# Attention in halves of 64 tokens on 64x64 parts of TensorE's array, in two visits a unit

## The chip, the cores and the metric

The kernel runs on one core of a Trainium2 chip. The metric is device time in microseconds (us). The kernel before took 674.11 us, the median of three runs (673.33 to 675.0).

A core has five engines that each work through their own instructions in order: PE (TensorE, matmuls; PEld are its weight loads), DVE (VectorE), ACT (ScalarE), POOL (GpSimd) and SP, which only issues DMAs here. ACT issues some DMAs too.

## The reference

Three layers follow each other: a linear attention with a decaying state (4 batch rows, 8 heads, 768 tokens, head size 48), a feed-forward layer with a maximum of three products, and a second one with a softmax and a layer norm. The change is in the first.

```python
for t in range(S):
    cur = np.einsum('bhd,bhe->bhde', u[None] * kt, vt)
    y[:, :, t] = np.einsum('bhd,bhde->bhe', rt, state + cur)
    state = wt[:, :, :, None] * state + np.einsum('bhd,bhe->bhde', kt, vt)
...
h = np.maximum(np.maximum(x @ w1, x @ w2), x @ w3);  x = h @ w_out
h = x @ w_in;  e = np.exp(h - h_max);  sm = e / (e.sum() + 1e-09)
solu = h * sm;  ln = (solu - mu) / np.sqrt(var + 1e-06) * g_ln;  out = ln @ w_out
```

## The kernel before

**Units.** The attention goes by 24 units, `u = 0..23`: 128 tokens of one batch row, all 8 heads, in 4 pairs `p` of 2 heads `e`. Units 0 to 3 are the first chunks of the four batch rows (`u // B == 0`), units 20 to 23 the last ones. Partitions 0 to 63 hold the even heads (48 rows used, padded to 64), 64 to 127 the odd ones.

**What a unit does.** DVE scans the products of `w` backwards (`s_sfx`, L265) and forwards (`s_pfx`, L283); POOL multiplies the first into `k` (L268), DVE the second into `r` (`s_rp`, L287). The diagonal (the term with `u`) comes from `s_rk` (POOL), `s_rku` and `s_diag` (DVE), and `s_dg` (POOL, L324) lays it out in two 128x512 tiles, one for each `e`. On PE:

- `s_score` (L336): 8 matmuls, 64 partitions by 128 key tokens by 128 query tokens, into two PSUM tiles. `s_mask` (DVE, L342, once for each `e`) copies what lies under the causal mask over the diagonal's tile.
- `s_y`: where there is a state, 8 matmuls of the decayed state `st` with `r` (L397, 64 by 64, 128 columns), and 8 of `v` with the masked scores (L401, all 128 key tokens by 64, 128 columns), in one accumulation. `s_yT` (ACT, L463) takes it out of PSUM.
- `s_state` (L418): 8 matmuls of the transposed `k` with `v` (128 tokens by 48, 64 columns), not for the last chunk. `s_sadd` adds them to the decayed state (DVE, L432, two instructions; for the first chunk two ACT copies, L434).

The transposed `k` comes from PE for units 0 to 4 (`s_kTp`) and from a DVE transpose and a round trip by DMA for later ones (`s_kq`, `s_kT`).

**Order.** All is issued in one order that is written out by hand. Units 0 to 3 stand in a loop of their own, mixed with the conversion of the first layer's weights (`conv`: three ACT, two DVE and some POOL instructions a piece; L195 and L199 are DVE's). From unit 4 on, each unit is a list of 12 items (`unit_items`), and `run_groups` deals the items out between groups of 9 matmuls of the first feed-forward layer (`stage_a` L526, `stage_b` L545), by PE time. After each 9 of L526, DVE or ACT must take the result out of one of 4 PSUM buffers (`ps_m`); the attention has 4 more (`ps_a`). So PE leaves the feed-forward matmuls three times for each unit: for the scores, for `s_y`, and for `s_state`. After the attention comes the second layer (L777, L854).

fp32 matmuls (the attention's) appear as two records each in the trace; those of the feed-forward layers, in float32r, as one.

Of the kernel before, what the change touches and what calls it, by code (L numbers as in the profile page):

```python
# [15 lines left out]
L = 128  # L16
NC_ = T // L
# [25 lines left out]
FMW = 2 * NP * L + NP * WB  # L43
# [26 lines left out]
def emit(tc, general, flag, fm, tm, ub, wa, win, wo2, g, cst, lmask, out):  # L70
# [7 lines left out]
    with ExitStack() as top:  # L78
# [5 lines left out]
        mask = cs[:, 0:128]  # L84
        ident = flat(x2)[:, KX * NU * L - 128:]
        ps_m = top.enter_context(tc.tile_pool(name="ps_m", bufs=4, space=PS))
        ps_a = top.enter_context(tc.tile_pool(name="ps_a", bufs=4, space=PS))
# [11 lines left out]
        a1 = attn.enter_context(tc.tile_pool(name="a1", bufs=1, side="right"))  # L99

        fm_t, rk_t, v_t, at = {}, {}, {}, {}
        xt, xf = {}, {}

        def parts(u):
            t = fm_t[u]
            p3 = lambda x: x.rearrange("p (a b) -> p a b", a=NP)
            return p3(t[:, 0:NP * L]), p3(t[:, NP * L:2 * NP * L]), t[:, 2 * NP * L:]

        def load_f(u, eng=A):
            """The rows between the heads hold constants that stay in a buffer once they are in it."""  # L110
            if u < NU and u not in fm_t:
                fresh = u < (2 if general else 3)
                fm_t[u] = fbuf[u % 2 if general else u if u < 3 else (u - 3) % 2]
                if u == 0:
                    eng.dma_start(parts(u)[2], fm[u][:, 2 * NP * L:])
                    eng.dma_start(fm_t[u][:, 0:2 * NP * L], fm[u][:, 0:2 * NP * L])
                elif fresh:
                    eng.dma_start(fm_t[u], fm[u])
                else:
                    for o in (0, 64):  # L120
                        eng.dma_start(fm_t[u][o:o + D], fm[u][o:o + D])

        def load_rk(u, eng=A):
            if u < NU and u not in rk_t:
                tag = dict(tag="kq", bufs=1) if u == 2 and not general else dict(tag="tm")
                rk_t[u] = apool.tile([128, 2 * DM], F32, name=f"rk{u}", **tag)
                eng.dma_start(rk_t[u], tm[u][:, 0:2 * DM])

        def load_v(u, eng=A):
            if u < NU and u not in v_t:  # L130
                tag = dict(tag="st", bufs=1) if u == 2 and not general else dict(tag="v")
                v_t[u] = apool.tile([128, H * DV], F32, name=f"v{u}", **tag)
                eng.dma_start(v_t[u], tm[u][:, 2 * DM:])
# [5 lines left out]
        fbuf = [a1.tile([128, FMW], F32, name=f"fm{i}") for i in range(2)] + [flat(x2)[:, SPARE:SPARE + FMW]]  # L139
# [14 lines left out]
        for s in sbd:  # L154
            G.memset(s, 0.0)

# [103 lines left out]
        def s_sfx(u):  # L260
            """Products of w over the tokens after each one, into k."""
# [46 lines left out]
        def a_tile(u, e):  # L308
            if not general and u in (1, 3):
                o = SPARE + FMW + e * NP * L  # L310
                return flat(x2)[:, o:o + NP * L].rearrange("p (a b) -> p a b", a=NP)
            return apool.tile([128, NP, L], F32, tag=f"a{e}", bufs=1, name=f"a{e}_{u}")

        def s_dg(u):
            d = at[u]
            for e in range(2):
                s = bc_last(d["s"].rearrange("p (a b) -> p a b", b=2)[:, :, e], L)
                if general:
                    t = apool.tile([128, NP, L], F32, tag="kq", bufs=1, name=f"dg{e}_{u}")
                    V.tensor_tensor(t, bc_mid(ident, NP), s, op=ALU.mult)  # L320
                    V.tensor_tensor(d["a", e], d["a", e], t, op=ALU.add)
                else:
                    d["a", e] = a_tile(u, e)
                    G.tensor_tensor(d["a", e], bc_mid(ident, NP), s, op=ALU.mult)  # L324

        def s_score(u):
            d = at[u]
# [10 lines left out]
        def s_mask(u, e):  # L338
# [3 lines left out]
            V.copy_predicated(d["a", e], bc_mid(mask.bitcast(I32), NP), d["sc", e])  # L342
# [43 lines left out]

        def s_y(u):
# [4 lines left out]
            s = sbd[u % B] if general else d.get("st")  # L392
# [15 lines left out]

        def s_state(u):
            d = at[u]  # L410
            if u // B == NC_ - 1:
                return
            v = v_t[u]
            d["ds"] = ps = pool_of(u).tile([128, NP, DV], F32, tag=pool_tag(u), name=f"ds{u}")
# [5 lines left out]

        def s_sadd(u):
            d = at[u]
            if u // B == NC_ - 1:
                return
            if general and u // B:
                G.tensor_tensor(sbd[u % B], sbd[u % B], bc_last(d["ptot"], DV), op=ALU.mult)
            for e in range(2):
                o = 64 * e
                dst = sbd[u % B][o:o + D]
                if u // B:  # L430
                    old = dst if general else d["st"][o:o + D]
                    V.tensor_tensor(dst, d["ds"][o:o + D], old, op=ALU.add)  # L432
# [3 lines left out]
        def s_kq(u):  # L436
            if NPT <= u < NU - B:
# [5 lines left out]
        def s_kT(u):  # L443
            if u < NU - B:
# [4 lines left out]
        pool_of = lambda u: ps_m if u < B else ps_a  # L449
        pool_tag = lambda u: "m" if u < B else "a"  # L450

        def s_kTp(u):
            if u < NPT:
                s_kT(u)
                ps = pool_of(u).tile([128, NP, L], F32, tag=pool_tag(u), name=f"kTp{u}")
# [4 lines left out]
        def s_yT(u):  # L460
            ps = at[u]["yp"]
            xf[u] = x = apool.tile([128, NP, L], F32, tag="xf", bufs=1, name=f"xf{u}")
            A.activation(x, ps, AF.Copy)  # L463
# [22 lines left out]
        def unit_items(u):  # L486
            n = u + 1
            nx = lambda f: f(n) if n < NU else None
            return [
                lambda: general and (s_diag(u), s_dg(u)),  # L490
                lambda: (s_score(u), s_kTp(u), s_decay(u)),
                lambda: (s_mask(u, 0), s_mask(u, 1), load_t(u + 1)),
# [7 lines left out]
                lambda: general or nx(s_diag),  # L500
                lambda: (general or nx(s_dg), n >= NPT and nx(s_kT)),
            ]

# [72 lines left out]
        def second_weights():  # L576
            """Ends the attention, with the check of the range of w, and sets up the last weights in its place."""
# [7 lines left out]
            attn.close()  # L585
            w2 = right.enter_context(tc.tile_pool(name="w2", bufs=1, side="right"))
# [19 lines left out]
        nc.sync.dma_start(cs, cst[:, 0:128])  # L606
# [11 lines left out]
        end_of = []  # L618
        for u in range(NU):
            items += unit_items(u)  # L620
            end_of.append(len(items) + 4)
        items += [lambda: None] * 3 + [lambda: s_xt(NU - 1)] + [lambda: None] * LEAD
# [34 lines left out]
        for u in range(B):  # L657
# [17 lines left out]
            if l >= 0:  # L675
# [7 lines left out]
            grp(GRP[u][0])  # L683
            s_y(u)
            conv.dve()
            if l >= 0:
# [12 lines left out]
        s_state(B - 1)  # L699
        s_sadd(B - 1)  # L700
        if general:
            for f in (s_sfx, s_pfx, s_rp, s_rk, s_rku):
                f(B)
        pos = end_of[B - 1] - 4
# [7 lines left out]
        def run_groups(groups, k0, k1, extra=(), ahead=1.0):  # L712
            """Emits MoE groups with attention items k0..k1 and the extra steps spread over them by PE time."""
# [181 lines left out]
def build(tc, fm, tm, ub, wa, win, wo2, g, cst, lmask, out):  # L895
    nc = tc.nc
    args = (fm, tm, ub, wa.bitcast(I32), win.bitcast(I32), wo2.bitcast(I32), g, cst, lmask, out)
# [10 lines left out]
def layout(r, k, v, w, u, moe_w1, moe_w2, moe_w3, moe_w_out, moe2_w_in, moe2_w_out, moe2_g_ln):  # L908
# [30 lines left out]
    cst = np.concatenate([i[:, None] < i[None, :], i[:, None] == i[None, :]], axis=1).astype(f32)  # L939
    lm = []  # L940
# [4 lines left out]
    d = dict(fm=fm, tm=tm, ub=ub, wa=wa, win=win, wo2=wo2, g=g, cst=cst, lmask=lmask)  # L945
# [17 lines left out]
```

## Time and profile before

| | us |
|---|---|
| median of the runs | 674.11 |
| profiled execution, span | 672.6 |
| PE busy | 627.4 (93%) |
| DVE busy | 469.3 (70%) |
| POOL busy | 416.3 (62%) |
| ACT busy | 300.3 (45%) |
| mean granted TensorE clock | 0.974 of full speed |

The profile is one execution on the chip. Busy times of PE are from the modelled ends of pipelined matmuls, so where it is busy all the time only the distance from one start to the next tells what an instruction costs. The granted clock is 1.0 or 0.5 in the records, 2.4 or 1.2 GHz.

### The profile page before, as it was taken

How to read it: one execution, taken by the hardware profiler on the slowest of the kernel's cores; microseconds unless marked ns; L12 is line 12 of the kernel's file. 1: busy time of each engine (PE TensorE's matmuls, PEld its weight loads, DVE VectorE, ACT ScalarE, POOL GpSimd, SP SyncE). 2: the span in 40 equal slices, each digit the busy share in tenths (PEclk: the TensorE clock that was granted, in tenths of full speed). 3: DMA queues.
4: the chain of work that ended last, by engine and by line, in shares of the span. 5: the costliest groups of instructions: out<-in, count | busy, mean ns of one | idle time of the engine just before them, and what ended most of it. 6: DMA issues, size and time to landing. Idle time of an engine off the chain costs nothing.

```text
span 672.6 us, 13761 instructions
## 1 busy us (share of the span) xinstructions
PE 627.4 (93%) x5038; PEld 582.1 (87%) x5038; DVE 469.3 (70%) x835; ACT 300.3 (45%) x738; POOL 416.3 (62%) x571
## 2 busy tenths in 40 slices
PE   1648898999999999999999999999999999999996
PEld 1537787999999999999999999999899999999996
DVE  8996889556688877776666562466877777777750
ACT  3565676122434434322222223475655555555542
POOL 6775678544566655565545553276877777777762
PEclk9877798999999999999999999999999999999998
DMA  9844571644465555455543330330577666676661
GB/s 343 212 121 122 175 176 44 153 110 109 109 144 133 135 146 125 117 111 109 110 110 78 79 80 7 95 99 32 127 156 163 158 150 150 137 160 149 146 153 54
DMA packets 158205, 85.57 MB, mean 127 GB/s; under 512 B 132048, under 2 KB 139984, under 8 KB 158128
## 3 DMA queue, kind: packets, MB, share of 16 engines
q1 hardware_dynamic: 149392, 58.37, 36.1%
q10 hardware_dynamic: 8736, 26.22, 15.3%
q8 instruction: 42, 0.69, 0.4%
q14 instruction: 35, 0.29, 0.2%
HBM read 62.68 MB, written 20.71 MB: 124 GB/s over the span
## 4 chain that ended last, share of the span: by engine, by line
PE 84%; DVE 6%; DMA 3%; issue 2%; ACT 2%; POOL 1%; SPq 1%; ACTq 0%; DVEq 0%
PE a L526 32%; PE h L777 15%; PE o L854 15%; PE b L545 11%; PE y L401 3%; PE sc L336 3%; PE y L397 3%; PE ds L418 1%; DMA v<-in_tm_dram 1%; DVE x L199 1%; DMA rk<-in_tm_dram 1%; DVE x L195 1%; DVE pf L283 1%; DMA fm<-in_fm_dram 1%; DVE sf L265 1%
## 5 line engine op out<-in xcount | busy, mean ns | idle before, releaser
L526 PE MATMUL a<-xh,wah 128*128 128x256 f32 x594 | 173.1, 291 | 1.7 <-DVE t L533 1.7
L526 PE MATMUL a<-xh,wal 128*128 128x256 f32 x594 | 168.8, 284 | 1.4 <-POOL wal L209 1.4
L526 PE MATMUL a<-xl,wah 128*128 128x256 f32 x594 | 168.7, 284 | 0.0
L533 DVE TENSOR_TENSOR t<-a,t 128x256 f32<-128x256 f32 x144 | 60.2, 418 | 92.0 <-PE a L526 70.8
L536 POOL TENSOR_TENSOR h<-t,h 128x256 fp32r<-128x256 f32 x66 | 55.9, 847 | 107.4 <-ACT h L535 103.8
L526 PEld LDWEIGHTS a<-xh,wah 128*128 128x128 f32 x594 | 114.3, 192 | 6.8 <-issue 2.0
L526 PEld LDWEIGHTS a<-xh,wal 128*128 128x128 f32 x594 | 114.4, 193 | 1.8 <-POOL wal L209 1.8
L526 PEld LDWEIGHTS a<-xl,wah 128*128 128x128 f32 x594 | 114.5, 193 | 0.1
L854 PE MATMUL o<-wo,lh 128*128 128x384 f32 x368 | 94.0, 337 | 0.0
L535 ACT ACTIVATE h<-t 128x256 fp32r<-128x256 f32 x66 | 27.5, 417 | 147.0 <-DVE t L533 141.1
L777 PE MATMUL h<-wi,x2h 128*128 128x512 f32 x288 | 90.7, 396 | 0.0
L846 POOL TENSOR_TENSOR ll<-c,lh 128x512 fp32r<-128x512 f32 x44 | 64.7, 1491 | 22.1 <-ACT lh L845 22.1
L545 PE MATMUL b<-h,wbh 128*128 128x256 f32 x396 | 73.6, 287 | 0.0
L854 PEld LDWEIGHTS o<-wo,lh 128*128 128x128 f32 x368 | 66.9, 189 | 1.8
L545 PEld LDWEIGHTS b<-h,wbh 128*128 128x128 f32 x396 | 61.8, 192 | 2.0 <-issue 1.0
L777 PEld LDWEIGHTS h<-wi,x2h 128*128 128x128 f32 x288 | 53.7, 189 | 10.9
L854 PE MATMUL o<-wo,ll 128*128 128x384 f32 x184 | 62.0, 337 | 0.0
L324 POOL TENSOR_TENSOR a<-x,s 128x512 f32<-128x512 f32 x44 | 47.6, 1103 | 18.0 <-DVE s L306 18.0
L777 PE MATMUL h<-wi,x2l 128*128 128x512 f32 x144 | 57.0, 396 | 0.0
L545 PE MATMUL b<-h,wbl 128*128 128x256 f32 x198 | 56.2, 284 | 0.5 <-POOL wbl L209 0.5
L793 ACT ACTIVATE e<-h,sm 128x512 f32<-128x512 f32 x48 | 32.6, 684 | 52.1 <-DVE sm L788 52.0
L794 DVE SCALAR_TENSOR_TENSOR p<-h,e 128x512 f32<-128x512 f32 x48 | 32.6, 691 | 20.3 <-ACT e L793 20.3
(134 smaller groups left out, 1337.8 us busy)
## 6 DMA issues: line engine op xcount, KB each, us to landing
fm<-in_fm_dram ACTq DMA_DIRECT2D x42, 289.5 KB, 5.1
pd<-q SPq DMA_DIRECT2D x23, 512.0 KB, 2.9
c<-pd SPq DMA_DIRECT2D x92, 128.0 KB, 3.8
x<-in_wa_dram SPq DMA_DIRECT2D x24, 384.0 KB, 3.8
rk<-in_tm_dram ACTq DMA_DIRECT2D x21, 384.0 KB, 3.6
v<-in_tm_dram ACTq DMA_DIRECT2D x21, 256.0 KB, 4.3
out_dram<-os SPq DMA_DIRECT2D x24, 192.0 KB, 3.2
kd<-kq SPq DMA_DIRECT2D x15, 256.0 KB, 3.8
```

Source lines behind the costliest of these rows:

```text
L324: G.tensor_tensor(d["a", e], bc_mid(ident, NP), s, op=ALU.mult)
L336: PE.matmul(d["sc", e][:, p], k3[o:o + 64, p], r3[o:o + 64, p], start=True, stop=True)
L526: PE.matmul(ps, w_[:, f, m, k], x_[:, k], start=(i == 0), stop=(i == 8))
L533: V.tensor_tensor(t, ps, t, op=ALU.max)
L535: A.activation(hh[:, f], t, AF.Copy)
L536: G.tensor_tensor(hl[:, f], t, hh[:, f].bitcast(F32), op=ALU.subtract)
L545: PE.matmul(ps, w_[:, f, m * 128:(m + 1) * 128], h_[:, f], start=(f == 0 and i == 0), stop=(f == KF1 - 1 and i == 2))
L777: PE.matmul(ps, x_[:, k], w_[:, k, b * 512:(b + 1) * 512], start=(n_ == 0), stop=(n_ == 8))
L793: A.activation(e[:, sl], d["h"][b], AF.Exp, bias=col(0), accum_out=col(2 + b))
L794: V.scalar_tensor_tensor(p[:, sl], d["h"][b], 1.0, e[:, sl], op0=ALU.mult, op1=ALU.mult, accum_out=col(4 + b))
L846: G.tensor_tensor(ll[:, b], c[:, b], lh[:, b].bitcast(F32), op=ALU.subtract)
L854: PE.matmul(ps, l_[:, k], w_[:, k], start=(n_ == 0), stop=(n_ == 3 * KF2 - 1))
```

## The change

Each unit is cut in halves `j` of 64 tokens. The score of a half against itself is 64x64, so each of the four combinations of `e` (rows of the array) and `j` (columns) is a matmul of its own on a 64x64 part, 64 columns long. What the second half needs of the first no longer stands in the scores: it goes through a second state `st1`, which is the decayed state plus the first half's `k` and `v`. `s_intra` (scores with `v`), `s_state2` and `s_inter` (state with `r`) take the place of `s_y` and `s_state`. In the items of a unit, `s_inter(u-1)` and `s_score(u)` stand together, and `s_intra(u)` and `s_state(u)` stand together.

The diagonal's tile is 128x512 once instead of twice, and so is the mask. `s_state2` is also done for the last chunk (first half only), with its transposed `k`. The loads of `r`, and of `k` and `w`, are two DMAs over all 128 partitions (before: two over 48 partitions each), issued at the third item of a unit instead of the tenth; `s_kq` moves from the ninth to the fourth item, `s_kT` from the twelfth to the eighth. The PSUM pool `ps_a` becomes two pairs of banks, `s` (scores, then state) and `y`, each with one buffer. The mask and the small identity come in one constant `half_cst`.

```diff
         def s_score(u):
-            for e in range(2):
-                d["sc", e] = ps_a.tile([128, NP, L], F32, tag="a", name=f"sc{e}_{u}")
+            d["sc"] = sc = pair("s", f"sc{u}")
             for p in range(NP):
-                for e in range(2):
-                    o = 64 * e
-                    PE.matmul(d["sc", e][:, p], k3[o:o + 64, p], r3[o:o + 64, p], start=True, stop=True)
+                for j in range(2):
+                    t = slice(j * HL, (j + 1) * HL)
+                    for e in range(2):
+                        o = slice(64 * e, 64 * e + 64)
+                        PE.matmul(sc[64 * j:64 * j + 64, e, p], k3[o, p, t], r3[o, p, t], start=True, stop=True)
...
+        def s_intra(u):
...
+            d["yp"] = y = pair("y", f"y{u}")
+            for p in range(NP):
+                for j in range(2):
+                    for e in range(2):
+                        h = 2 * p + e
+                        o = slice(64 * j, 64 * j + 64)
+                        PE.matmul(y[64 * e:64 * e + 64, j, p], v[o, h * DV:(h + 1) * DV], d["a"][o, h],
+                                  start=(p == 0), stop=(c == 0 and j == 0 and p == NP - 1))
+
+        def s_inter(u):
...
+            for j in range(0 if u // B else 1, 2):
+                s = d["st1"] if j else d["st"]
+                for p in range(NP):
+                    for e in range(2):
+                        o = slice(64 * e, 64 * e + 64)
+                        PE.matmul(d["yp"][o, j, p], s[o, p], rt[o, p, j * HL:(j + 1) * HL],
+                                  start=False, stop=(p == NP - 1))
...
+        def s_state2(u):
...
+            d["ds"] = ds = pair("s", f"ds{u}")
+            for p in range(NP):
+                for j in range(1 if u // B == NC_ - 1 else 2):
+                    o = slice(64 * j, 64 * j + 64)
+                    for e in range(2):
+                        h = 2 * p + e
+                        PE.matmul(ds[64 * e:64 * e + 64, j, p], d["kT"][o, p, 64 * e:64 * e + 64],
+                                  v[o, h * DV:(h + 1) * DV], start=True, stop=True)
...
+        def s_sadd2(u):
...
+            d["st1"] = st1 = apool.tile([128, NP, DV], F32, tag="st1", bufs=1, name=f"st1_{u}")
+            if u // B:
+                V.tensor_tensor(st1, d["ds"][:, 0], d["st"], op=ALU.add)
+            else:
+                A.activation(st1, d["ds"][:, 0], AF.Copy)
+            if u // B < NC_ - 1:
+                V.tensor_tensor(sbd[u % B], d["ds"][:, 1], st1, op=ALU.add)
...
+                return [
+                    lambda: (u > B and s_inter(u - 1), s_score(u), s_kTp(u)),
+                    lambda: (s_mask(u), u > B and s_yT(u - 1), s_decay(u), nx(s_sfx)),
+                    lambda: load_f(u + 2),
+                    lambda: (s_intra(u), s_state(u), nx(s_kq), u == B and s_xt(u - 1)),
+                    lambda: (s_sadd(u), load_t(u + 1)),
...
             s_dg(m)
-            s_mask(u, 0)
-            s_mask(u, 1)
+            s_mask(u)
+            grp(GRP[u][0])
+            if general:
+                s_y(u)
+            else:
+                s_intra(u)
+                s_state(u)
+                s_sadd(u)
+                s_inter(u)
```

The first place is PE around unit 6, in the stretch where the items are dealt out. Before, the scores (`sc`), the output (`y`, first with the state `st`, then with `a` and `v`) and the state (`ds`) stand apart, with feed-forward matmuls where lines are left out:

```order
L336 MATMUL sc_6_1283<-fm_97 128x128
L336 MATMUL sc_6_1284<-fm_97 128x128
...
L397 MATMUL y_1354<-fm_97,st_1293 64x128 x8
L401 MATMUL y_1354<-a_6_1239,v_993 64x128
L401 MATMUL y_1354<-a_6_1241,v_993 64x128
...
L418 MATMUL ds_1424<-v_993,kT_1243 48x64 x8
```

On PE at the same place of the changed program, with unit 6's output `y_1489`; the next unit's scores are `sc_1688`:

```order
L424 MATMUL y_1150<-fr_98,st_5_1219 64x64 x8
L350 MATMUL sc_1411<-fr_96,fk_100 64x64 x16
...
L412 MATMUL y_1489<-a_1380,v_1224 64x64 x16
L458 MATMUL ds_1506<-v_1224,kT_1296 64x64 x16
...
L424 MATMUL y_1489<-fr_96,st_1449 64x64 x8
L424 MATMUL y_1489<-fr_96,st_6_1544 64x64 x8
L350 MATMUL sc_1688<-fr_97,fk_99 64x64 x16
```

Three places became two; the second and third matmul of a unit now stand together, and the one with the state follows a unit's length later, in front of the next scores.

The second place is DVE in unit 1, in the loop of the first four units. Before, the two masks are followed by the conversion (`x`) and the next unit's scan (`sf`):

```order
L306 TENSOR_REDUCE s_270<-rk_136 128x8
L342 COPY_PREDICATED x_66<-cs,sc_1_224 128x512
L342 COPY_PREDICATED x_66<-cs,sc_1_225 128x512
L195 SCALAR_TENSOR_TENSOR x_66<-x_66 128x384
L199 SCALAR_TENSOR_TENSOR x_66<-x_66 128x384
```

On DVE of the changed program at that place (`sbd` is the state that the next chunk reads, `st_1` is `st1` of unit 1):

```order
L315 TENSOR_REDUCE s_307<-x_66 128x8
L357 COPY_PREDICATED x_66<-cs,sc_263 128x2x4x64
L484 TENSOR_TENSOR sbd_115<-ds_329,st_1_346 128x256
L204 SCALAR_TENSOR_TENSOR x_66<-x_66 128x384
L208 SCALAR_TENSOR_TENSOR x_66<-x_66 128x384
```

One mask is gone, and an addition stands in its place that reads what PE and then ACT make from that mask's result.

## Rows read from the trace of the kernel before

**Rows 1.** The page: busy us of each engine, its share of the span, instructions.

```profile
PE 627.4 (93%) x5038; PEld 582.1 (87%) x5038; DVE 469.3 (70%) x835; ACT 300.3 (45%) x738; POOL 416.3 (62%) x571
```

**Rows 2.** Stretches: length, busy of PE, PEld, DVE, ACT, POOL, clock, DMA share, GB/s.

```profile
0.00:60.00 60.00, 29.34 (x241) 24.08 (x243) 53.68 (x69) 29.59 (x64) 40.59 (x37) 0.83 0.66 198
60.00:124.50 64.50, 56.09 (x480) 52.17 (x479) 50.84 (x82) 40.94 (x96) 46.71 (x43) 0.92 0.57 145
124.50:409.00 284.50, 284.50 (x2828) 269.11 (x2827) 197.98 (x339) 91.60 (x257) 157.51 (x165) 1.00 0.47 112
409.00:672.60 263.60, 257.49 (x1499) 236.75 (x1497) 166.76 (x346) 138.19 (x323) 171.46 (x327) 0.99 0.52 123
```

**Rows 3.** PE in order of time, a visit for scores: start, us, instruction, tiles.

```profile
244.01 0.28 PE L526 MATMUL a<-xh,wal 128*128 128x256 f32 x1
244.22 1.16 PE L336 MATMUL sc<-fm 64*128 64x128 f32 x16
245.31 0.39 PE L526 MATMUL a<-xh,wah 128*128 128x256 f32 x1
245.53 0.28 PE L526 MATMUL a<-xl,wah 128*128 128x256 f32 x1
245.65 0.28 PE L526 MATMUL a<-xh,wal 128*128 128x256 f32 x1
```

**Rows 4.** The same view, a visit for the output.

```profile
248.53 0.28 PE L526 MATMUL a<-xh,wal 128*128 128x256 f32 x1
248.74 1.09 PE L397 MATMUL y<-fm,st 64*64 64x128 f32 x16
...
250.78 0.39 PE L526 MATMUL a<-xh,wah 128*128 128x256 f32 x1
251.00 0.28 PE L526 MATMUL a<-xl,wah 128*128 128x256 f32 x1
```

**Rows 5.** The same view, a visit for the state.

```profile
271.25 0.28 PE L545 MATMUL b<-h,wbl 128*128 128x256 f32 x1
271.46 0.65 PE L418 MATMUL ds<-v,kT 128*48 128x64 f32 x16
272.04 0.51 PE L545 MATMUL b<-h,wbh 128*128 128x256 f32 x2
272.38 0.28 PE L545 MATMUL b<-h,wbl 128*128 128x256 f32 x1
```

**Rows 6.** The same view: 128 columns on the whole array; two records of one column.

```profile
656.97 1.04 PE L838 MATMUL pT<-ident,p 128*128 128x128 f32 x8
...
438.40 0.19 PE L756 MATMUL flp<-fl 128*1 128x1 f32 x2
```

**Rows 7.** Groups of PE: the mean length of one of those two records, in ns.

```profile
L756 PE MATMUL flp<-fl 128*1 128x1 f32 x2 | 0.2, 164 | 0.0
```

**Rows 8.** Stretches, the sum from 18.3 to 53.4 us.

```profile
sum 35.10, PE 19.32 PEld 15.55 DVE 34.69 ACT 18.83 POOL 25.39; mean PE 6.44 PEld 5.18 DVE 11.56 ACT 6.28 POOL 8.46
```

**Rows 9.** In order of time, unit 1 in the first loop: DVE, POOL, PE.

```profile
27.47 1.32 DVE L342 COPY_PREDICATED x<-cs,sc 128x512 f32<-128x512 int32 x2
28.69 0.54 DVE L195 SCALAR_TENSOR_TENSOR x<-x 128x384 int32<-128x384 int32 x1
...
30.47 1.35 DVE L195 SCALAR_TENSOR_TENSOR x<-x 128x384 int32<-128x384 int32 x1
...
27.70 2.43 POOL L324 TENSOR_TENSOR a<-x,s 128x512 f32<-128x512 f32 x2 [1.75 <-DVE s L306]
...
32.76 1.09 PE L418 MATMUL ds<-v,kT 128*48 128x64 f32 x16
```

**Rows 10.** Groups, the state's addition on DVE and its copy on ACT.

```profile
L432 DVE TENSOR_TENSOR sbd<-ds,st 48x256 f32<-48x256 f32 x32 | 13.2, 411 | 1.0 <-PE ds L418 0.8
...
L434 ACT ACTIVATE sbd<-ds 48x256 f32<-48x256 f32 x8 | 3.0, 375 | 1.2 <-PE ds L418 0.7 <-DMA x<-in_wa_dram 0.5
```

**Rows 11.** Stretches, four units with much work on DVE.

```profile
193.70:260.00 66.30, 66.30 (x667) 62.46 (x666) 55.23 (x96) 27.59 (x82) 39.68 (x45) 1.00 0.61 143
```

More of the change, by code (lines that the diff above doesn't have):

```diff
@@ L16 @@
 L = 128
+HL = L // 2
 NC_ = T // L
@@ L130, in load_v @@
             if u < NU and u not in v_t:
-                tag = dict(tag="st", bufs=1) if u == 2 and not general else dict(tag="v")
-                v_t[u] = apool.tile([128, H * DV], F32, name=f"v{u}", **tag)
+                if u == 2 and not general:
+                    v_t[u] = spare(FMW + H * HL + 2 * DM, H * DV)
+                else:
+                    v_t[u] = apool.tile([128, H * DV], F32, tag="v", name=f"v{u}")
                 eng.dma_start(v_t[u], tm[u][:, 2 * DM:])
@@ L137, in load_t @@
             load_v(u)
-        fbuf = [a1.tile([128, FMW], F32, name=f"fm{i}") for i in range(2)] + [flat(x2)[:, SPARE:SPARE + FMW]]
+        rbuf = [a1.tile([128, NP * L], F32, name=f"fr{i}") for i in range(2 if general else 3)]
+        kwbuf = [a1.tile([128, FMW], F32, name=f"fk{i}") for i in range(2)] + [spare(0, FMW)]
         u_sb = a1.tile([128, DM], F32, name="u_sb")
@@ L153, in emit @@
         sbd = [a1.tile([128, NP, DV], F32, name=f"sbd{i}") for i in range(B)]
-        for s in sbd:
-            G.memset(s, 0.0)
+        if general:
+            for s in sbd:
+                G.memset(s, 0.0)
         class Conv:
@@ L391, in s_y @@
             v = v_t[u]
-            s = sbd[u % B] if general else d.get("st")
+            s = sbd[u % B]
             d["yp"] = ps = ps_a.tile([128, NP, L], F32, tag="a", name=f"y{u}")
@@ L407, in s_decay @@
                 G.tensor_tensor(tmp, sbd[u % B], bc_last(at[u]["ptot"], DV), op=ALU.mult)
+        def s_state2(u):
+            d = at[u]
+            v = v_t[u]
+            d["ds"] = ds = pair("s", f"ds{u}")
[6 more added lines that the diff above has]
+                                  v[o, h * DV:(h + 1) * DV], start=True, stop=True)
         def s_state(u):
             d = at[u]
+            if not general:
+                return s_state2(u)
             if u // B == NC_ - 1:
@@ L430, in s_sadd @@
                 if u // B:
-                    old = dst if general else d["st"][o:o + D]
-                    V.tensor_tensor(dst, d["ds"][o:o + D], old, op=ALU.add)
+                    V.tensor_tensor(dst, d["ds"][o:o + D], dst, op=ALU.add)
                 else:
@@ L462, in s_yT @@
             xf[u] = x = apool.tile([128, NP, L], F32, tag="xf", bufs=1, name=f"xf{u}")
-            A.activation(x, ps, AF.Copy)
+            if general:
+                A.activation(x, ps, AF.Copy)
+            else:
+                A.activation(x.rearrange("p a (j t) -> p j a t", j=2), ps, AF.Copy)
             for k in range(KX):
@@ L488, in unit_items @@
             nx = lambda f: f(n) if n < NU else None
+            if not general:
+                return [
[4 more added lines that the diff above has]
+                    lambda: (s_sadd(u), load_t(u + 1)),
+                    lambda: (nx(s_pfx), u > B and s_xt(u - 1)),
+                    lambda: nx(s_rp),
+                    lambda: (nx(s_stat), n >= NPT and nx(s_kT)),
+                    lambda: nx(s_rk),
+                    lambda: nx(s_rku),
+                    lambda: nx(s_diag),
+                    lambda: nx(s_dg),
+                ]
             return [
-                lambda: general and (s_diag(u), s_dg(u)),
+                lambda: (s_diag(u), s_dg(u)),
                 lambda: (s_score(u), s_kTp(u), s_decay(u)),
-                lambda: (s_mask(u, 0), s_mask(u, 1), load_t(u + 1)),
+                lambda: load_t(u + 1),
                 lambda: (nx(s_sfx), s_xt(u - 1)),
@@ L499, in unit_items @@
                 lambda: (s_sadd(u), nx(s_rku), load_f(u + 2)),
-                lambda: general or nx(s_diag),
-                lambda: (general or nx(s_dg), n >= NPT and nx(s_kT)),
+                lambda: None,
+                lambda: n >= NPT and nx(s_kT),
             ]
@@ L618, in emit @@
         end_of = []
+        TAIL = 4 if general else 6
         for u in range(NU):
             items += unit_items(u)
-            end_of.append(len(items) + 4)
-        items += [lambda: None] * 3 + [lambda: s_xt(NU - 1)] + [lambda: None] * LEAD
+            end_of.append(len(items) + TAIL)
+        if general:
+            items += [lambda: None] * 3 + [lambda: s_xt(NU - 1)]
+        else:
+            items += [lambda: s_inter(NU - 1), lambda: s_yT(NU - 1)] + [lambda: None] * 3 + [lambda: s_xt(NU - 1)]
+        items += [lambda: None] * LEAD
         pos = 0
@@ L674, in emit @@
             s_rku(m)
-            if l >= 0:
+            if general and l >= 0:
                 s_state(l)
```

110 lines of the change are left out of this document (63 added, 47 removed).

## The prediction

> **What bounds the kernel now.** I read the page first: PE is busy 93% of the span, no other engine over 70% [rows 1]. A share over the whole hides stages, so the stretches come next [rows 2]. In the first 60 us DVE is busy 53.68 and PE 29.34; from 18.3 to 53.4 DVE works 34.69 of 35.10 [rows 8]. From 60 to 124.5 PE (56.09 of 64.50) and DVE (50.84) share the bound. From 124.5 to 409 PE is busy 284.50 of 284.50: what PE does in the attention is on the path to the end, one for one. After 409 the second layer begins to take over, which the change leaves alone. So the change is worth what it does to PE in the third stretch, less what it does to DVE in the first.
>
> Since ends of matmuls are modelled, a visit's price is read from starts: from the last feed-forward matmul before it to the second one after it (the first starts late), less the steps of 0.12 that those take anyway (245.53 to 245.65). Scores: 245.53 − 244.01 − 0.24 = 1.28 [rows 3]. Output: 251.00 − 248.53 − 0.24 = 2.23 [rows 4]. State: 272.38 − 271.25 − 0.36 = 0.77 [rows 5]. A unit costs PE 4.28; the last four, without the state, 3.51.
>
> **How a visit's price is made up.** Each fp32 matmul is two records. On the whole array eight records of 128 columns span 1.04; the scores' sixteen, on two halves of rows, span 1.16, and the output's sixteen on two 64x64 parts 1.09 [rows 3, 4, 6]. So two parts run at once, and a slot is one record on each. The output has eight slots of 128 columns more than the scores and costs 0.95 more, 0.119 a slot with a change of array shape in it; so a slot of 64 columns is about 0.06. The state is eight such slots, 0.48; its remaining 0.29 is what entering and leaving cost.
>
> **PE after the change.** `s_inter` has 16 matmuls on two parts: 16 slots of 64 columns. `s_score`, `s_intra` and `s_state2` have 16 matmuls each (8 in two parts for the last chunk's state); if four parts run at once, 8 slots each. First visit: 0.29 + 24 × 0.06 = 1.73. Second: 0.29 + 16 × 0.06 = 1.25. Together 2.98.
>
> - Units 6 to 19, all in the third stretch: 14 × (4.28 − 2.98) = 18.2.
> - Units 20 to 23: 4 × (3.51 − 2.98) = 2.1; the last `s_inter` is a visit of its own, 0.29 back. Together 1.8.
> - Units 4 and 5 lie where PE shares the bound: half of 2 × 1.30 = 1.3.
>
> Gain 21.3. The unknown is a slot with four parts. No row shows four at once. Bounds: 0.06, as two parts cost, and 0.12, if two is the most. I take 0.06: pairs of parts that share columns (scores) and pairs on the diagonal (L397) run without slowing each other [rows 3, 4]. Each 0.01 more costs 24 slots × 14 units + 16 × 4, that is 4.0 us.
>
> Two records of one column on the same part stand 0.19 − 0.164 = 0.026 apart [rows 6, 7], and the state's sixteen, on two parts, average 0.03 or more [rows 5]. So the rows leave open whether 0.026 is a limit of a part or of all PE. The Trainium skill ("TensorE: Matmul & The Clock Gate", "Wait — 56ns, not 53.3ns?") gives start to start never below about 25 ns, however few the columns; as a limit of PE it would make a four-part slot 0.10, take 16 us from the gain and leave an end near 672. The same page ("The mechanism" of packing) has records on different parts start about 4 ns apart, which no row here shows for more than two; by that the slot stays 0.06.
>
> **Waits on PE.** `s_intra` waits for the mask and, as `y` has one buffer, for ACT's `s_yT(u-1)`; both are issued two items earlier, with three groups of L526 between the visits, some 3.2 us, as now between scores and output (245.31 to 248.53) [rows 3, 4]. DVE's mask is one instruction of 0.66 instead of two [rows 9], so it ends sooner. Queued behind `s_intra` are the state and all feed-forward matmuls. `s_inter` waits for `st1`, made some seven items before: nothing.
>
> **Other engines, third stretch.** DVE loses 0.66 a unit (one mask); its additions are two of 0.41 as before [rows 10]; four more units get a transpose. POOL loses one of two L324, about 1.2 [rows 9]. The heaviest four units have DVE busy 55.23 of 66.30 [rows 11]: 13.2 a unit after, against 15.3 of PE, 86%. Hidden. DMAs: `load_f` moves 128 instead of 96 partitions, a third more, with as many issues on ACT; it is issued seven items earlier, in front of `load_t` in ACT's queue, and its buffers are free once the scores are done. On SP `s_kq` and `s_kT` come earlier, behind the permuting DMAs of `s_yT`; units 20 to 23 add a write and four reads each. With DMA share 0.47 [rows 2] and four items or more until each is used, nothing. If one lands late, ACT or SP stands, and PE has three PSUM buffers, some 3 us, before it notices.
>
> **First 60 us.** For units 0 to 3 the chain is new: mask (DVE), intra and state (PE), `st1` (ACT), `sbd` (DVE). On DVE the `sbd` addition waits for all of it, and behind it stand the conversion and the next unit's scan; on ACT, behind `st1`, the loads three units ahead and the next conversion; on PE, behind `s_inter`, only the next scores, and PE is idle there anyway. At half clock the state's sixteen records span 1.09 [rows 9], so intra and state, eight slots each like it, take about 2.0; ACT takes 0.38 [rows 10] and I allow 0.3 for hand-overs: DVE stands 2.7, then adds 0.41, less a mask of 0.66. Full price 2.4 a unit, 9.8 for four. Against it: DVE's L195 takes 0.54 once and 1.35 another time, the long ones while POOL works on [rows 9]. In the new wait POOL does its diagonal (one instead of two) and `rk` alone, and DVE's three long conversions and the scan behind it come back by up to 0.8 each, 2.4 or more. Bounds per unit: 0 and 2.4. I take 0.8, nearer to the covered end, since most of POOL's 2.43 and what follows it falls into the wait: 3 in all, and later visits start 3 later.
>
> **Sum.** −18.2 − 1.8 − 1.3 + 3 = −18.3. The profiled execution has 672.6; the median is 1.5 above it, which I take as around both alike: 654.3 for the span, 655.8 for the median. I forecast 655.5.
>
> **Rivals.**
>
> 1. *Two parts are the most PE runs at once.* A four-part slot is then 0.12, six more hundredths, 24 us: 674.1 − 18.3 + 24 = 680, slower. For: no row has more than two, and four need four weight loads in a slot. Against: both kinds of pairs run unslowed. It turns slower once the slot is over 0.06 + 18.3/4.0 × 0.01 = 0.106. Chance 0.10.
> 2. *PE starts no record sooner than 0.026 after another*, whichever part: slot 0.104, costs 17.6, ends at 673.5, no change. For: the two records of rows 6. Against: these two are on one part, where the second also has to wait for the first. Chance 0.07.
> 3. *DVE's new wait in the first loop is not covered*: 9.8 instead of 3, ends at 662.6. For: DVE has no idle time there [rows 8]. Against: the slowed conversions. Chance 0.12.
> 4. *DVE becomes the bound in the heavy units* (7 to 14), where mask, scans and additions now stand closer: half of eight units' 1.30 is lost, 661. For: 86% is near. Against: four PSUM buffers. Chance 0.05.
>
> The forecast has 0.63; 0.03 is left for what I don't see. The forecast's own range, with 0.055 to 0.065 for the slot and 0 to 6 for the start, is 650 to 661. Rivals 3 and 4 lie just above it; the range 647 to 669 takes them in and leaves out rivals 1 and 2 and little else, so it holds about 8 in 10. A measurement of this kernel can tell 0.3%, 2 us. Faster: forecast, rivals 3 and 4, a third of rival 2: 0.83. Same: the rest of rival 2 and a little of rival 1: 0.06. Slower: 0.11.
>
> **What would show it.** In the third stretch, two visits a unit that cost together about 3.0 by the same reading, with a score's 32 records within some 0.7: step right; over 0.9 and visits 0.3 to 1.0 longer: rival 2 (0.104 a slot) or 1 (0.12). PE still busy all of that stretch: rival 4 wrong; idle before L526 released by DVE: right. In the first loop, DVE's wait before `sbd` of 2 to 3, and conversions of 0.55 after it: covered; conversions still of 1.35 behind such a wait: rival 3. My forecast is wrong if a unit's visits cost above 3.4, or if PE stands idle in the third stretch for more than 5 us.

## The result and the profile after

The changed kernel takes 663.39 us (663.23 to 663.99) against 674.07, a ratio of 0.9842 with a 95% interval of 0.9829 to 0.9856. It is faster by 10.7 us, where 18.3 were forecast. It lies inside the range of 647 to 669, but above the forecast's own range of 650 to 661. The profiled execution has a span of 661.5.

The page's line of busy time after, as [rows 1], shows PE with 23.5 us less work in more and shorter records:

```profile
PE 603.9 (91%) x6574; PEld 568.4 (86%) x6574; DVE 446.4 (67%) x823; ACT 297.8 (45%) x734; POOL 388.4 (59%) x543
```

The stretches, with the columns of [rows 2]. The third is cut at 397.7, 11.3 sooner, as the second layer starts that much sooner; PE is no longer busy all of it: 269.84 of 273.20. In the second, PE is less busy than before and DVE more.

```profile
0.00:60.00 60.00, 23.72 (x482) 20.99 (x482) 43.73 (x65) 26.63 (x59) 28.90 (x28) 0.75 0.59 202
60.00:124.50 64.50, 52.86 (x621) 48.98 (x621) 52.77 (x84) 40.98 (x96) 44.24 (x41) 0.94 0.51 156
124.50:397.70 273.20, 269.84 (x3938) 261.59 (x3937) 183.99 (x330) 91.37 (x256) 144.42 (x150) 1.00 0.49 137
```

A unit's two visits in order of time, read as [rows 3 to 5] were:

```profile
254.53 0.28 PE L607 MATMUL a<-xh,wal 128*128 128x256 f32 x1
254.75 1.08 PE L424 MATMUL y<-fr,st 64*64 64x64 f32 x29
...
255.72 0.64 PE L350 MATMUL sc<-fr,fk 64*64 64x64 f32 x30
256.29 0.39 PE L607 MATMUL a<-xh,wah 128*128 128x256 f32 x1
256.51 0.28 PE L607 MATMUL a<-xl,wah 128*128 128x256 f32 x1
...
259.51 0.28 PE L607 MATMUL a<-xh,wal 128*128 128x256 f32 x1
259.72 0.69 PE L412 MATMUL y<-a,v 64*64 64x64 f32 x32
260.23 0.65 PE L458 MATMUL ds<-v,kT 64*64 64x64 f32 x32
260.81 0.39 PE L607 MATMUL a<-xh,wah 128*128 128x256 f32 x1
261.03 0.28 PE L607 MATMUL a<-xl,wah 128*128 128x256 f32 x1
```

First visit: 256.51 − 254.53 − 0.24 = 1.74. Second: 261.03 − 259.51 − 0.24 = 1.28. Together 3.02 (forecast 2.98) instead of 4.28. The 32 records of L412 span 0.69; if the last takes some 0.22, as a lone record of this form does, the starts are 0.47/31 = 0.015 apart.

To see where the rest went, PE's records of the feed-forward (L607 and L626; L526 and L545 before; the same sequence in both) are counted as steps of 0.12 us. Whatever a step takes beyond 0.12 is a visit (attention records lie in it) or idle; up to step 360, idle also holds what steps at the lower granted clock take longer. These times, worked out from the starts in both traces, count from a zero that is some 0.24 us later than that of the views:

| steps | before: visits, idle | after: visits, idle | difference |
|---|---|---|---|
| first step at | 45.5 | 46.2 | +0.7 |
| 0 to 360 (to 121.6; to 126.0) | 22.0, 11.1 | 19.8, 17.0 | +3.8 |
| 360 to 2200 | 74.2, 1.3 | 53.2, 5.3 | −17.0 |
| 2200 to the second layer | 0, 0.2 | 1.3, 0.2 | +1.3 |
| second layer starts at | 457.8 | 446.5 | −11.3 |

Three things stand in it: visits saved 19.7 in units 6 to 23 (forecast 20.0), PE stands 4.0 more in the same stretch (the 1.3 before are small remainders of steps: no stand there is over 0.15), and step 360 comes 4.4 later where the forecast had +1.7 (3 for the first loop, less 1.3). These two are 6.7 us, about what is missing. The profile's waits of PE name the releasers, from 124 to 405 us (us in total, times, longest):

```profile
PE a L607 <- POOL xl L550: 1.5, 2, 0.8
PE b L626 <- POOL wbl L218: 0.6, 1, 0.6
PE a L607 <- ACT xh L549: 0.5, 2, 0.3
```

and ACT's waits in that stretch have one that is new:

```profile
ACT xh L549 <- DMA xf<-xf: 9.9, 4, 6.1
```

The chain of waits around 169 us (start, us, what) puts them in order:

```profile
164.00 4.76 DMA xf<-xf
...
168.86 0.53 ACT xh L549
169.39 0.07 issue
169.46 1.00 POOL xl L550
```

The last of `s_yT`'s permuting DMAs is issued at 164.00 and lands 4.8 later; `s_xt` splits its result into `xh` and `xl`; PE, which starts a new tile with them, has to wait. It stands for `xh` and `xl` at 168.8 (0.50 and 0.95 beyond a step) and again at 202.7 (0.36 and 1.10). The second time the DMAs were issued from 195.75 to 196.94 and landed within 1.8, and it is ACT's own queue that holds `xh`: ACT issues four loads from 199.56 on and then does a conversion, with no pause before `xh`:

```profile
202.36 0.35 ACT L200 ACTIVATE x<-x 128x192 int32<-128x192 f32 x1
202.61 0.51 ACT L549 ACTIVATE xh<-xf 128x384 fp32r<-128x384 f32 x1
```

The two tile starts are 2.9 of the 4.0. POOL's conversion `wbl` (0.8, at 127.5) and smaller stands make up the rest.

### The profile page after: what moved, and what is told of

Read it like the earlier page. It is cut to its first block, busy times and chain, and to the rows that moved or that the text cites. A ratio compares the mean times of both kernels' runs of the same rounds, so it can differ in the third digit from the quotient of the medians.

```text
span 661.5 us, 16814 instructions
## 1 busy us (share of the span) xinstructions
PE 603.9 (91%) x6574; PEld 568.4 (86%) x6574; DVE 446.4 (67%) x823; ACT 297.8 (45%) x734; POOL 388.4 (59%) x543
## 4 chain that ended last, share of the span: by engine, by line
PE 77%; DVE 2%; POOL 1%; DMA 1%; issue 1%; ACT 1%; ACTq 0%; SPq 0%; DVEq 0%
PE a L607 30%; PE h L870 15%; PE o L947 15%; PE b L626 9%; PE y L424 3%; PE y L412 2%; PE sc L350 1%; PE ds L458 1%; DMA xf<-xf 1%; DVE t L614 0%; DVE sf L274 0%; POOL xl L550 0%; DVE x L204 0%; DVE a L357 0%; DVE x L208 0%
## 5 line engine op out<-in xcount | busy, mean ns | idle before, releaser
L607 PE MATMUL a<-xh,wah 128*128 128x256 f32 x594 | 173.1, 291 | 2.7 <-ACT t L611 2.0
L607 PE MATMUL a<-xh,wal 128*128 128x256 f32 x594 | 168.7, 284 | 2.2 <-POOL wal L218 2.2
L607 PE MATMUL a<-xl,wah 128*128 128x256 f32 x594 | 168.7, 284 | 1.5 <-POOL xl L550 1.5
L607 PEld LDWEIGHTS a<-xh,wah 128*128 128x128 f32 x594 | 114.3, 192 | 6.4 <-ACT t L611 2.6
L607 PEld LDWEIGHTS a<-xh,wal 128*128 128x128 f32 x594 | 114.3, 192 | 2.8 <-POOL wal L218 2.8
L607 PEld LDWEIGHTS a<-xl,wah 128*128 128x128 f32 x594 | 114.4, 193 | 1.9 <-POOL xl L550 1.9
L617 POOL TENSOR_TENSOR h<-t,h 128x256 fp32r<-128x256 f32 x66 | 59.8, 907 | 94.3 <-ACT h L616 82.3
L626 PE MATMUL b<-h,wbh 128*128 128x256 f32 x396 | 73.1, 285 | 2.2 <-DVE t L614 2.2
L626 PEld LDWEIGHTS b<-h,wbh 128*128 128x128 f32 x396 | 61.8, 192 | 3.3 <-DVE t L614 2.4
L626 PE MATMUL b<-h,wbl 128*128 128x256 f32 x198 | 56.1, 283 | 0.6 <-POOL wbl L218 0.6
L550 POOL TENSOR_TENSOR xl<-xf,xh 128x384 fp32r<-128x384 f32 x22 | 28.8, 1307 | 30.0 <-ACT xh L549 27.1
```

The costliest lines, as they stand in the source:

```text
L550: G.tensor_tensor(xl[:, :, o:o + L], x[:, 0:KX], xh[:, :, o:o + L].bitcast(F32), op=ALU.subtract)
L607: PE.matmul(ps, w_[:, f, m, k], x_[:, k], start=(i == 0), stop=(i == 8))
L617: G.tensor_tensor(hl[:, f], t, hh[:, f].bitcast(F32), op=ALU.subtract)
L626: PE.matmul(ps, w_[:, f, m * 128:(m + 1) * 128], h_[:, f], start=(f == 0 and i == 0), stop=(f == KF1 - 1 and i == 2))
```

## The experiments

Times are medians; those of the changed kernel's variants are to be held against 663.4. The runs of one variant spread by 0.8 to 6.1 us, so besides the time I read four marks of each trace, worked out as in the table above. A trace is of one execution, which can lie up to 1.7 us off the median, and up to step 360 the stretches in which the granted clock is 0.50 differ from trace to trace. (Where expectations give PE's idle as 4.4 after and 0.84 before, they go by another count than the table's 5.3 and 1.3.)

| kernel | time | ratio to before, 95% | first step | step 360 | idle 360 to 2200 | second layer |
|---|---|---|---|---|---|---|
| changed | 663.4 | 0.9842 (0.9829 to 0.9856) | 46.2 | 126.0 | 5.3 | 446.5 |
| two parts | 675.6 | 1.0015 (1.0006 to 1.0025) | 48.6 | 130.1 | 3.1 | 459.0 |
| sbd later | 661.6 | 0.9809 (0.9795 to 0.9822) | 43.4 | 123.8 | 4.9 | 443.8 |
| s_xt later | 658.8 | 0.9763 (0.9745 to 0.9780) | 46.0 | 123.7 | 2.1 | 440.7 |
| lead 3 | 659.9 | 0.9779 (0.9758 to 0.9800) | 46.2 | 126.3 | 1.6 | 443.2 |
| both | 655.5 | 0.9722 (0.9706 to 0.9738) | 43.8 | 121.9 | 1.9 | 439.0 |
| before, s_xt later | 679.9 | 1.0085 (1.0070 to 1.0100) | 45.7 | 127.9 | 0.4 | 462.4 |
| s_xt(4) alone | 664.3 | 0.9859 (0.9834 to 0.9883) | 46.0 | 128.5 | 5.1 | 448.8 |
| rku later | 661.1 | 0.9801 (0.9788 to 0.9815) | 46.5 | 123.7 | 5.6 | 444.3 |

**Two parts at a time.**

```diff
-            for p in range(NP):
-                for j in range(2):
+            for j in range(2):
+                for p in range(NP):
```

(in `s_score`, `s_intra` and `s_state2` alike)

> The changed kernel took 663.4. Here the loops over j and p change places in scores, intra and state, so that runs of 16 records keep to two array parts; nothing else moves. Theory (four parts work at once, a slot of 64 columns stays 0.06, as the visits of the changed kernel, 1.74 + 1.28, suggest): 24 slots more a unit, 24 x 0.06 = 1.44, the visits go to 1.74 + 0.48 = 2.2 and 1.28 + 0.96 = 2.2; with 14 units in full and 4 of 16 slots on PE's bound stretch 20.2 + 3.8 = 24, so 687, slower than before. Rival (two parts at once are all that PE runs, and the visits became short for another reason, such as fewer changes of shape): visits stay at 3.0 and the time at 663 to 664.

675.6: the whole gain is gone, so the gain hangs on four parts at work at once, and the rival falls. But 12.2 came, not 24. PE in order of time in this kernel shows why:

```profile
250.64 0.80 PE L412 MATMUL y<-a,v 64*64 64x64 f32 x26
251.23 0.27 PE L458 MATMUL ds<-v,kT 64*64 64x64 f32 x2
251.27 0.28 PE L412 MATMUL y<-a,v 64*64 64x64 f32 x3
251.34 0.22 PE L458 MATMUL ds<-v,kT 64*64 64x64 f32 x1
```

Records of the state (L458) start ahead of the last of intra (L412), on the other two parts. Single records show the same inside intra: those on the second pair of parts begin at 250.93, while the last on the first pair start at 251.10. Each change of pair thus overlaps by about 0.17. The second visit has three such changes and grows from 1.28 to 1.69 (1.39 in units 20 to 23), not by 0.96; the first grows from 1.74 to 2.03, not by 0.48.

**The addition into sbd behind the conversion (first loop).**

```diff
             conv.dve()
+            if not general:
+                s_sbd(u)
```

(`s_sbd` is the addition into `sbd`, taken out of `s_sadd2` where u < B)

> In the first four units DVE's addition into sbd is put behind the conversion that follows it, so that DVE no longer stands 2.5 to 2.6 a unit waiting for ACT's copy of the state; the rest is the changed kernel (663.4). Theory (the wait is covered up to the 3 us that the forecast gave it: unit 3's mask ended 0.8 later than before, the first feed-forward matmul came 0.7 later, 45 matmul steps on 4.4 later): 660 to 661.5. Rival A (the wait is not covered, and what follows it in units 4 to 6 is its price too, 4.5 with the missing 1.3): 658 to 659. Rival B (fully covered: the conversions just get slow again beside POOL, 1.35 for 0.55): 663 to 664.

661.6. DVE in unit 1, first in the changed kernel, then here (start, us, instruction, idle before it):

```profile
27.86 0.72 DVE L357 COPY_PREDICATED x<-cs,sc 128x512 f32<-128x512 int32 x1
31.29 0.43 DVE L484 TENSOR_TENSOR sbd<-ds,st 128x256 f32<-128x256 f32 x1 [2.72 <-ACT st L482]
31.63 0.55 DVE L204 SCALAR_TENSOR_TENSOR x<-x 128x384 int32<-128x384 int32 x1
32.10 0.55 DVE L208 SCALAR_TENSOR_TENSOR x<-x 128x384 int32<-128x384 int32 x1
```

```profile
27.51 0.72 DVE L357 COPY_PREDICATED x<-cs,sc 128x512 f32<-128x512 int32 x1
28.12 1.09 DVE L204 SCALAR_TENSOR_TENSOR x<-x 128x384 int32<-128x384 int32 x1
29.14 1.35 DVE L208 SCALAR_TENSOR_TENSOR x<-x 128x384 int32<-128x384 int32 x1
30.94 0.42 DVE L489 TENSOR_TENSOR sbd<-ds,st 128x256 f32<-128x256 f32 x1 [0.45 <-ACT st L482]
```

The wait shrinks from 2.72 to 0.45, but the two conversions that now lie in it, beside POOL's work, cost 2.44 instead of 1.10. Over the first 14 conversion instructions DVE spends 15.05 us before (9 of them over 0.9 us), 9.31 in the changed kernel (2) and 11.97 here (6). So the wait is mostly covered, as forecast; what it costs is 2.2 at step 360, 1.8 in the time, a little less than the theory of this run had.

**s_xt two items later, tiles two items later.**

```diff
-                    lambda: (nx(s_pfx), u > B and s_xt(u - 1)),
+                    lambda: nx(s_pfx),
                     lambda: nx(s_rp),
-                    lambda: (nx(s_stat), n >= NPT and nx(s_kT)),
+                    lambda: (nx(s_stat), n >= NPT and nx(s_kT), u > B and s_xt(u - 1)),
...
-        TAIL = 4 if general else 6
+        TAIL = 4 if general else 8
```

> s_xt(u-1) goes two items later, from item 6 to item 8, and each tile's feed-forward starts two items later with it, so that the permuting DMAs of s_yT (4.8 us at 164.0) have six items instead of four. Theory (the 1.07 and 1.22 that PE stands at the start of two tiles, at 168.6 and 202.9, are that chain: copy of y, DMAs, xh; ACT stands up to 6.1 in it): both go, idle of PE in the third stretch falls from 4.4 to about 2, time 660.5 to 661.5. Rival (the late xh is only where a delay that comes from DVE or POOL shows, and returns at another group): idle stays at 4 to 4.5, time within 0.7 of 663.4.

658.8, more than expected: idle in the third stretch falls by 3.2, and step 360 comes 2.3 sooner, which the theory does not explain (the last run below does). Of the 3.2, 1.0 returns as waits of PE in front of intra (second visits 1.37 on average instead of 1.31). PE's waits there, 124 to 405 us:

```profile
PE y L412 <- issue: 1.1, 1, 1.1
PE y L412 <- ACT xf L529: 0.2, 1, 0.2
PE a L607 <- POOL xl L550: 0.2, 1, 0.2
```

**The tiles alone later.**

```diff
-LEAD = 1
+LEAD = 3
```

> Each tile's feed-forward starts three items after its last s_xt instead of one; s_xt itself stays at item 6, four items behind s_yT, so ACT still waits for the permuting DMAs as long as now. Theory (what costs is that PE asks for xh too soon): as the run with s_xt two items later, 660.5 to 661.5. Rival (what costs is ACT standing in its queue before xh, which holds up its copies for PE): the waits of ACT on xf stay near 10 us in sum and PE's idle near 4, time within 0.7 of 663.4; the two runs then differ by 2 or more.

659.9. Idle falls as much (5.3 to 1.6, of which 1.4 returns before intra), while ACT still waits, though half as long:

```profile
ACT xh L549 <- DMA xf<-xf: 4.8, 5, 1.9
```

So it is the early demand of PE for `xh` that costs, not ACT's standing. The two times are not told apart by their intervals. Step 360 does not move here, but in this trace PE runs 28 steps shortly before it at 0.21 instead of 0.12, with the granted clock at 0.50 (1.2 GHz), where the changed kernel has 1.00 (this run, then the changed kernel, columns as in [rows 2]):

```profile
111.50:118.30 6.80, 6.08 (x28) 6.08 (x29) 5.63 (x11) 2.71 (x8) 4.12 (x4) 0.50 0.00 1
111.50:118.30 6.80, 5.57 (x41) 4.96 (x42) 5.72 (x9) 3.58 (x10) 4.84 (x6) 1.00 0.25 39
```

That is some 2.6 us. So this mark does not show that later tiles leave units 4 to 6 as they were.

**Both edits.**

> Both edits at once: the addition into sbd behind the conversion, and s_xt two items later with the tiles' start. Alone they gave 661.6 and 658.8 against the changed kernel's 663.4. Theory (two causes, one in the first loop, one at the tiles' starts): the gains add, 663.4 - 1.8 - 4.6 = 657.0, range 656 to 658. Rival (in units 4 to 6 both take up the same slack, since from there DVE sets the pace): 658.5 to 659.5, no better than the second alone.

655.5, faster than either alone and than both kernels: 7.9 below the changed kernel, where the sum is 6.4, and just under the theory's range. Step 360 is back at 121.9, as before the change.

**What PE's and DVE's time is worth, by stage.** Two runs repeat PE's matmuls, with J = 1 or 4, one repeats a transpose on DVE:

```diff
-                i = 0
+                for _ in range(2 if j == J and m == 1 else 1):
+                    i = 0
...
-                V.transpose(out=kq, in_=flat(parts(u)[1]))
+                for _ in range(3 if u < 7 else 1):
+                    V.transpose(out=kq, in_=flat(parts(u)[1]))
```

> The changed kernel, with the nine matmuls of six groups of the feed-forward's second tile (those that DVE's maximum reads first) done twice: 6 x 1.08 = 6.5 us more of PE between 70 and 110 us, where the forecast let half of PE's saving count. The result is the same. Forecast's half: 663.4 + 3.2 = 666.6. Theory now (in units 4 to 6 the conversions on DVE, ACT and POOL set the pace and PE's time counts for little): 663.4 to 665. Rival (PE's time counts in full, and its saving there was lost to something else): 669 to 670.

> The same six groups done twice, but in the fifth tile, some 205 to 235 us, in units of the third stretch: again 6 x 1.08 = 6.5 us of PE. Theory (there PE's time counts one for one): 663.4 + 6.5 = 669.9, from 669 to 670.5. Rival (DVE is near enough to its limit in units 7 to 14 that part of PE's time there is covered): 666 to 668.

> The changed kernel, with DVE's transpose of k for units 5 and 6 done three times into the same tile: 4 x 0.70 = 2.8 us more of DVE between 70 and 115 us; the result is the same. Theory (DVE sets the pace there): 663.4 + 2 to 3 = 665.5 to 666.5. Rival (DVE's idle, 15 of 80 us there, takes it up): 663 to 664.3.

Early PE: 666.2 (0.9867, 0.9845 to 0.9888). Late PE: 669.8 (0.9931, 0.9913 to 0.9950). Early DVE: 666.2 (0.9869, 0.9848 to 0.9890). By the medians these are 2.8 of 6.5, 6.4 of 6.5 and 2.8 of 2.8; by the ratios 1.7, 6.0 and 1.8. In the third stretch PE counts one for one or close to it. In units 4 to 6 the intervals of both early runs overlap the changed kernel's. That PE counts in full there is excluded (the ratio would be 0.9938); the forecast's half and my theory of "little" are not told apart. That DVE counts for more of its time than PE does is likely, but not shown.

**The kernel before with s_xt later.** The edit moves `s_xt(u - 1)` for units above 4 from the item of `s_sfx` to that of `s_rp` and each tile's start by two items.

> The kernel before, with s_xt(u-1) two items later for units above 4 and each tile's feed-forward two items later with it, as the run that gained 4.6 on the changed kernel. Theory (the change made the wait: it cut the items between s_yT and s_xt from nine to four, and PE's idle in the third stretch, 0.84 before, has nothing to give back): 673.0 to 675.0, no gain in the third stretch, at most 1 either way in units 4 to 6. Rival (two items more of lead help any version, the shortfall is not the change's): 669 to 671.

679.9, slower: the edit is no gain in itself. In the third stretch nothing changes (idle 0.4 against 1.3), as expected; but step 360 comes 6.3 later, six times what I allowed. PE now stands 2.46 for DVE's maximum (`t`), a wait that the kernel before does not have and the changed kernel does (here, then the changed kernel):

```profile
121.72 0.50 PE L545 MATMUL b<-h,wbh 128*128 128x256 f32 x2 [2.46 <-DVE t L533]
120.85 0.51 PE L626 MATMUL b<-h,wbh 128*128 128x256 f32 x2 [2.18 <-DVE t L614]
```

So in units 4 to 6 it matters where the items stand against the groups of feed-forward matmuls.

**Intra one item later**, on top of both edits: `s_intra`, `s_state` and `s_sadd` one item down, `nx(s_pfx)` one up.

> Both edits that gained (655.5 together), and intra with the state one item later, behind the next unit's prefix scan (s_inter does its second half first, which only changes the order of its matmuls). In the run with both edits PE still stood before intra at 93.1 (2.30), 216.9 (1.37), 233.4 (0.71) and 264.9 (0.48), for the mask and for ACT's copy of y. Theory (an item, 1.3 us or more, is enough for them): the three of the third stretch go, 2.2, and of the first one half counts, 1.0: 652 to 653.5. Rival (the state and both additions then come an item later, and DVE and the conversions lose in units 4 to 6 what PE gains): 655 to 657.

656.9 (0.9750, 0.9730 to 0.9770): no gain, the rival's range. Its profiled execution took 662.7, the longest of five, and alone has a granted clock of 0.50 for 6.8 us from 238.9, so its trace does not tell why.

**One s_xt.** `s_xt(4)` from item 6 to item 8, nothing else.

> The changed kernel with one call moved: s_xt(4), in unit 5, goes from item 6 to item 8 (in the trace of the changed kernel its copy stands at 109.9 and POOL's part of 1.37 at 110.5); all tiles start where they did. When every s_xt went two items later, PE reached its 360th feed-forward step 2.3 earlier; when the tiles alone started later, it did not (126.3 against 126.0). Theory (what units 4 to 6 lose beside the first loop's wait is the place of this one call in the queues of ACT and POOL): step 360 near 123.7, time 661 to 662. Rival (it is the place of other items against the groups, shifted by the two items more that run there): 126, time 663 to 664.

664.3, the rival's time and not the theory's. PE waits for DVE's maximum until 120.84, as in the changed kernel (120.85). Step 360 at 128.5 instead of 126.0 comes from what follows: the granted clock is 0.50 from 119.6 to 126.5 here. The theory falls: what the earlier run gained in units 4 to 6 is not this one call.

**The product of rk one item later.**

```diff
-                    lambda: nx(s_rku),
-                    lambda: nx(s_diag),
+                    lambda: None,
+                    lambda: (nx(s_rku), nx(s_diag)),
```

> The changed kernel with DVE's product behind POOL's square (s_rku) one item later, directly ahead of s_diag. In units 4 to 6 of the changed kernel the longest wait of PE, 2.46 at 118.2, ends with a chain: ACT's h, POOL's h (0.74), POOL's rk (0.97), DVE's rk that stood 1.8 for it and took 1.33, then DVE's maximum (0.42) that PE's stage waits for. Theory (what is lost there is DVE standing in its queue for a POOL step issued one item before): the maximum goes ahead of the rk product, the wait falls below 1, step 360 comes near 124 instead of 126.0, 661 to 662. Rival (DVE has as much to do there all the same, so that the wait comes back one or two groups on): 125.5 to 126.5 at step 360, 663 to 664.

661.1, step 360 at 123.7. DVE near 118 us in the changed kernel, then here:

```profile
116.78 0.55 DVE L208 SCALAR_TENSOR_TENSOR x<-x 128x384 int32<-128x384 int32 x1
119.13 1.33 DVE L309 TENSOR_TENSOR rk<-rk,u_sb 128x384 f32<-128x384 f32 x1 [1.80 <-POOL rk L305]
120.39 0.94 DVE L614 TENSOR_TENSOR t<-a,t 128x256 f32<-128x256 f32 x2
```

```profile
116.75 0.55 DVE L208 SCALAR_TENSOR_TENSOR x<-x 128x384 int32<-128x384 int32 x1
118.00 0.95 DVE L614 TENSOR_TENSOR t<-a,t 128x256 f32<-128x256 f32 x2 [0.70 <-ACT t L611]
119.10 1.35 DVE L309 TENSOR_TENSOR rk<-rk,u_sb 128x384 f32<-128x384 f32 x1
```

The maximum that PE waits for comes 2.39 sooner, and PE's wait there (2.18 in the view, 2.46 from one start to the next) is gone. This is the one chain in units 4 to 6 that is shown. In the kernel before, DVE's product stands behind the maximum too:

```profile
117.72 0.42 DVE L533 TENSOR_TENSOR t<-a,t 128x256 f32<-128x256 f32 x1 [0.49 <-PE a L526]
118.94 1.03 DVE L300 TENSOR_TENSOR rk<-rk,u_sb 128x384 f32<-128x384 f32 x1
```

The same wait is gone in both runs whose tiles start later: with `s_xt` two items later PE stands 0.22 there, with the tiles alone later not at all. There more items run before the same group, and DVE's product ends at 117.1 and 117.8 instead of 120.5. That accounts for the 2.3 that `s_xt` later gained at step 360.

## Why the prediction was right, and where it was not

The forecast was right about the gain on PE and took off too little for what the change costs. That 663.4 lies in the range is in part luck: it misses the forecast's own 650 to 661, and the range reaches that far only to take in rivals 3 and 4, neither of which happened. Rival 3 ends at 662.6, close to what was measured, for another reason.

- **Visits.** 3.02 a unit against 2.98; 19.7 saved in units 6 to 23 against 20.0. The slot of 64 columns stays 0.06 with four parts, as taken. Rival 1 falls with the visits, and the run with two parts at a time shows the gain hangs on four. Rival 2 falls too: records start 0.015 apart on average, below 0.026. The floor of about 25 ns that the Trainium skill gives ("TensorE: Matmul & The Clock Gate", "Wait — 56ns, not 53.3ns?") does not hold for all of PE here; this trace lets it stand at most for one part.
- **First loop.** The forecast allowed 3 for DVE's wait and expected 2 to 3 of it a unit, with conversions of 0.55 behind it. The trace has 2.72 and 0.55, and DVE reaches its 15th conversion at 60.8 instead of 58.4: 2.4. Moving the addition gave 2.2 at step 360. Rival 3, at full price, falls.
- **Units 4 to 6.** "Half of 2 × 1.30" treats the visits alone. PE's time does count for less than full there, 0.26 or 0.43 by the two readings. But the change also moved the items against the groups, and so put one of DVE's products, which waits for POOL, ahead of a maximum that PE waits for. The forecast had no term for that. It cost some 2.7 (4.4 at step 360 less the 1.7 forecast; up to 0.9 of that may be the clock, as steps at 0.50 lose 3.3 up to there after and 2.4 before), and 2.3 came back when that product was moved behind the maximum.
- **The step that failed** is, as the prediction put it, on DMAs: "four items or more until each is used, nothing", and with it "PE still busy all of that stretch". `s_yT` and `s_xt` were nine items apart before and are four apart now, and a tile starts one item after `s_xt`. In the first tile that was late the last DMA took 4.8, and PE had asked for `xh` by then; in the second, ACT's loads and conversion stood in front of `xh`. I counted the items for loads and for `kT`, but not for the output on its way to the feed-forward, the one transfer for which PE waits directly. Idle of PE rose by 4.0, 2.9 of it at the two tile starts (the forecast called itself wrong from 5 on; the 5.3 in the table hold the 1.3 that the kernel before has too). In the runs that start the tiles later 3.2 to 3.7 went, and 1.0 to 1.4 returned in front of intra.
- **Rival 4**, DVE as the bound in the heavy units, falls: PE's waits there are for `xh`, `xl` and one conversion by POOL, but for 0.5 before intra, and PE's added time counted 6.0 to 6.4 of 6.5.

Sum: 18.3 forecast; 4.0 less for PE standing in the third stretch, 2.7 less for units 4 to 6, 0.3 for the visits: 11.3, as the second layer starts 11.3 sooner; the median shows 10.7.

Open: which part of the new order put DVE's product ahead of the maximum in units 4 to 6 (in the kernel before, `s_xt` and the tiles two items later do it), how much of DVE's time counts there, and why intra one item later gives nothing. The run with both edits and the later product together was not tried.

## What to carry to other kernels

When an item moves, count the items to each consumer, and start with the transfer whose result the bounding engine reads itself: what had nine items of cover may have four. Price a stage by an added piece of work of known length on one engine at a time; with enough runs it says whether a saving there counts in full, in part or not at all. When a mark is read from a single trace, read the granted clock of that stretch beside it. Small matmuls that alternate over four 64x64 parts took half the time that as many took on two.

## What the hardware showed beyond that

Four 64x64 parts run twice the fp32 records of two in the same time: in the view after, 32 records of the state with `r`, on two parts, take from 254.75 to 255.72, and 32 of intra, on four, from 259.72 to 260.23. Where successive records lie on two parts only, records for the other two start out of their turn (251.23 before 251.27, above), and the loop order costs 12 us, not 24. DVE's conversion instruction takes 0.55 with POOL idle. All of the first 14 that take over 0.9 (up to 1.40) run beside POOL, though some beside POOL stay at 0.55. So a wait in which POOL finishes is in part given back: 5.7 us over these 14.
